# One-core attention and two dense blocks in float32: low words of the float64 weights in PSUM, FF rows in plain order, eight late products on GpSimd, refitted ranks

## The chip, the cores and the metric

The kernel runs on one core of a Trainium2 chip. The metric is the time of one execution on the device in microseconds (us). Three runs of the kernel before were timed, and one more execution was profiled. The engines are named as the profile names them: PE (TensorE), ACT (ScalarE), DVE (VectorE), POOL (GpSimd), SP (SyncE, which here only issues DMAs).

## The reference

```python
# q (1,12288,128), kv (1,384,32,128) float32; alpha (2048), a (4), b (2)
kv_pool = kv.reshape(B, H//4, 4, W//4, 4, C).mean(axis=(2, 4))      # 768 keys
k = v = kv_pool.reshape(B, -1, C) @ w_sr
s = (q @ k.T) / sqrt(C);  a_ = exp(s - max(s));  a_ /= sum(a_) + 1e-9
x = (a_ @ v).reshape(12288, 128)
h = x @ w_in                                                         # 128 -> 2048
x = (max(h, 0) + alpha * min(h, 0)) @ w_out                          # 2048 -> 128
h = x @ w_in2                                                        # 128 -> 2048
P = a[0] + a[1]*h + a[2]*h**2 + a[3]*h**3
Q = 1 + |b[0]|*|h| + |b[1]|*h**2
out = (P / (Q + 1e-6)) @ w_out2                                      # 2048 -> 128
```

The four weight matrices arrive as float64, 512 KB for each slice of 512 of the 2048 FF rows or columns; the rest is float32.

## The kernel before, in words

**Work.** The 12288 query rows are 96 attention tiles of 128. Four tiles make a chunk of 512 rows, which is what both dense blocks work on: 24 chunks, each of 16 steps of 128 FF columns per block. A product that must keep float32 precision is made by `mm3`: both operands are split in a high and a low part in a reduced format, and three matmuls are summed in PSUM.

**First block, a step** (`moe1`): three matmuls into a PSUM bank `h1`, ACT's relu, a split into `rh` and `rl` on ACT and POOL, and matmuls onto `acc1`. The part that is linear in x goes through one 128x128 matrix M, made from the weights once.

**Second block, a pair of steps** (`moe2`, 128x1024 where both steps go together): matmuls into two banks `h2`; `u = |h|` and `p1` on ACT; `t` and `t2` on POOL (Q - 1 by Horner's rule); `ln` and `ex` on ACT give r = 1/Q in the PSUM pair `rp`; on DVE `p2` and `p3` for each step, then `e` = Q r, `gr` = P r (its sign turned) and `g` = (e - 2) gr, a Newton step; PE then adds the two products of `g` to `acc2`. `gr` is written over r in `rp`, which one pair at a time can hold.

**Weights.** `f64_to_f32` takes a float64 slice as pairs of 32-bit words. ACT makes a magnitude of the high words (`mag`) and a float of the low words (`low`, into a buffer `lf`); DVE clamps, shifts, joins the sign (`join`), takes the exponent, scales `lf` with it (`scale`) and adds (`final`). There are 16 slices: four each of w_in and w_out of both blocks. For a w_in slice, ACT and DVE then make the high and the low part (`hi`, `lo`). For the first block PE also transposes the w_in slice and multiplies it with the w_out slice for M; that goes through a PSUM bank `m` with one buffer, which the pooling of kv and the transposes of q use as well. Loads go through a ring `ld` of seven buffers.

**Start.** kv comes in 12 loads of 512 KB. DVE adds pairs of rows, PE pools them by matmuls (L496), and two matmuls (L528) make the keys, of which ACT and DVE write the high and low part (`kTh`, `kTl`, L537). Then the first 12 tiles of attention (`EARLY`) run with wider buffers.

**Order.** All work is first listed as operations with an engine, a cost, a rank and their dependencies. `emit_in_time` then plays a list schedule: on each engine the operation that can start first by the planner's costs is emitted, ties by rank. Buffers are rings whose users are linked in order of rank. What it emits is the fixed order of each engine's queue; on the chip each engine takes its queue in that order and waits by semaphores. The ranks come from tables of numbers (`WR`, `TR`, `RK`, `LH` and others).

Of the kernel before, what the change touches and what calls it, by code (L numbers as in the profile page):

```python
# [196 lines left out]
def kernel(  # L197
# [28 lines left out]
    RT = 11.07  # L226
    RA = 12.85
    RB = 105.28
    SPREAD = 38.43
    WLO = "DVE"  # L230
# [22 lines left out]
    NE = "POOL"  # L253
    NL = "POOL"
    SCL = "DVE"
    FIN = "DVE"
    RK = dict(
        relu=-90.72, G2a=26.46, u=4.12, p1=-20.09, t=-74.51, ln=78.89, ex=26.27, e=150.58, p2=25.63, p3=18.07, gr=-75.87, g=21.27, G2b=19.62, gs=13.78, q=27.79,
# [77 lines left out]
    first = units((("pooled", 2), ("ld", 2), ("bits", 2), ("w", 2), ("wo", 1), ("lf", 1)))  # L336
# [64 lines left out]
    with tc.manual_schedule():  # L401
# [12 lines left out]
        nc.gpsimd.dma_start(out=al.rearrange("p (g k) -> p g k", k=4), in_=moe_alpha.rearrange("(g p k) -> p g k", p=P, k=4))  # L414
# [6 lines left out]
        def queries(c, rank, ring):  # L421
# [38 lines left out]
            ld = add("SP", 1.6 if by_dve else 0.8, rank - 20, load)  # L460
# [128 lines left out]
        def f64_to_f32(src, order, dst, rank, dst_ring=None):  # L589
# [45 lines left out]
            def scale():  # L635
                TT[SCL].tensor_tensor(
# [11 lines left out]
            ld = add("SP", 1.5, rank - 10, load)  # L648
# [3 lines left out]
            lw = add("ACT", act_us(CH, True), rank, low, ld)  # L652
            d_lf = rings["lf"].take(lw)
# [22 lines left out]
        def prep_wo(n, w, g, rank):  # L676
# [4 lines left out]
            def dst():  # L681
# [827 lines left out]
```

## Time and profile before

| | us |
|---|---|
| median of 3 runs | 1550.62 (1547.54 to 1551.07) |
| the profiled execution | 1551.88, of it the span on the core 1549.8 |
| PE busy in the span | 1495.5 (97%) |
| DVE busy | 1448.8 (93%) |
| ACT busy | 1417.3 (91%) |
| POOL busy | 1314.0 (85%) |

Mean granted TensorE clock 0.991. All shares are averages over a start, a long middle and an end, which have different limits. A matmul row overlaps the next, so a mean duration on PE is longer than the distance between starts; on DVE and ACT too a row begins some 0.08 us before the one ahead of it has ended.

### The profile page before, as it was taken

To read this page: it belongs to the slowest core of one execution; us is meant where nothing else is said; L and a number is where in the kernel's file an instruction comes from. 1 tells how busy PE (TensorE), PEld (TensorE's weight loads), DVE (VectorE), ACT (ScalarE), POOL (GpSimd) and SP (SyncE) were. 2 spreads that over 40 slices of the span, in tenths; PEclk is the share of its full clock that TensorE was granted. 3 is DMA by queue.
4 is the path that set the end of the run, shared out by engine and by line. 5 is a ranking of instruction groups with operands and counts; after the bars stand their busy time and mean duration, and the time that the engine had idled before them with its cause. 6 is when DMAs were issued, how large, how long until landed. Compare 5 with 4: busy or idle time off the path is not lost.

```text
span 1549.8 us, 20219 instructions
## 1 busy us (share of the span) xinstructions
PE 1495.5 (97%) x6372; PEld 1074.5 (69%) x6372; DVE 1448.8 (93%) x2171; ACT 1417.3 (91%) x2465; POOL 1314.0 (85%) x1007
## 2 busy tenths in 40 slices
PE   6979999999999999999999999999999999999985
PEld 5866777777777777777777777776777776767642
DVE  6995899999999999999999999999999999999997
ACT  3867999999999999999999999999999999999974
POOL 0456999998999999989999889999899998989763
PEclk9999999999999999999999999999999999999998
DMA  8310000000000000000000000000000000000000
GB/s 274 121 36 1 8 7 8 14 1 15 14 1 15 8 8 8 14 8 15 7 8 15 3 12 8 8 14 7 8 14 7 1 8 7 1 8 7 4 11 7
DMA packets 99211, 28.64 MB, mean 18 GB/s; under 512 B 92929, under 2 KB 95505, under 8 KB 99105
## 3 DMA queue, kind: packets, MB, share of 16 engines
q1 hardware_dynamic: 98976, 27.28, 7.5%
q8 instruction: 50, 0.82, 0.2%
q0 software_dynamic: 128, 0.08, 0.1%
q14 instruction: 57, 0.46, 0.1%
HBM read 21.05 MB, written 6.29 MB: 18 GB/s over the span
## 4 chain that ended last, share of the span: by engine, by line
PE 86%; DVE 7%; ACT 4%; POOL 1%; issue 1%; DMA 1%; SPq 0%; DVEq 0%; ACTq 0%
PE acc L1267 19%; PE h L378 11%; PE h L380 11%; PE h L379 11%; PE acc L1138 6%; PE acc L378 4%; PE acc L380 4%; PE acc L379 4%; PE S L378 4%; PE S L379 4%; PE S L380 4%; PE S L882 3%; PE m L496 1%; DVE work L1234 1%; DVE rp L1228 1%
## 5 line engine op out<-in xcount | busy, mean ns | idle before, releaser
L1191 POOL TENSOR_TENSOR work<-work 128x1024 f32<-128x1024 f32 x192 | 461.2, 2402 | 6.4
L1267 PE MATMUL acc<-work,wo 128*128 128x512 f32 x768 | 393.5, 601 | 18.7 <-DVE work L1234 18.7
L1177 ACT ACTIVATE work<-h,nav 128x512 f32<-128x512 f32 x384 | 316.4, 828 | 19.8 <-PE h L380 17.1
L1122 POOL TENSOR_TENSOR rl<-work,rh 128x512 fp32r<-128x512 f32 x216 | 281.6, 1304 | 39.5 <-ACT rh L1113 36.0
L1184 POOL TENSOR_SCALAR work<-work,bab 128x1024 f32<-128x1024 f32 x192 | 231.3, 1205 | 77.1 <-ACT work L1172 58.5
L1217 DVE TENSOR_TENSOR work<-work,h 128x512 f32<-128x512 f32 x384 | 259.2, 681 | 30.8 <-ACT work L1172 29.1
L1221 DVE SCALAR_TENSOR_TENSOR work<-work,nav,h 128x512 f32<-128x512 f32 x384 | 283.2, 743 | 3.1
L1211 DVE SCALAR_TENSOR_TENSOR work<-work,rp 128x1024 f32<-128x1024 f32 x192 | 233.7, 1217 | 24.8 <-ACT rp L1204 22.0
L1172 ACT ACTIVATE work<-h 128x512 f32<-128x512 f32 x384 | 247.8, 654 | 2.5 <-POOL work L1191 2.0
L1228 DVE SCALAR_TENSOR_TENSOR rp<-work,nav,rp 128x1024 f32<-128x1024 f32 x192 | 246.3, 1283 | 0.0
L1234 DVE SCALAR_TENSOR_TENSOR work<-work,rp 128x1024 f32<-128x1024 f32 x192 | 233.4, 1215 | 2.1
L1101 ACT ACTIVATE work<-h 128x512 f32<-128x512 f32 x336 | 216.3, 644 | 19.7 <-PE h L380 14.2
L1196 ACT ACTIVATE work<-work 128x1024 f32<-128x1024 f32 x192 | 215.2, 1121 | 11.9 <-POOL work L1191 10.0
L1204 ACT ACTIVATE rp<-work 128x1024 f32<-128x1024 f32 x192 | 207.9, 1083 | 9.9 <-DVE work L1234 8.1
L378 PE MATMUL h<-x,w1h 128*128 128x512 f32 x384 | 201.3, 524 | 1.1 <-DVE rl L1105 0.6
L378 PE MATMUL h<-x1h,w2h 128*128 128x512 f32 x384 | 189.8, 494 | 1.1 <-DVE work L1221 1.0
L1267 PEld LDWEIGHTS acc<-work,wo 128*128 128x128 f32 x768 | 139.0, 191 | 66.7 <-DVE work L1234 24.9
L901 POOL TENSOR_TENSOR aTl<-tf,aTh 128x384 fp32r<-128x384 f32 x168 | 170.8, 1021 | 9.2 <-ACT tf L383 9.1
L380 PE MATMUL h<-x1h,w2l 128*128 128x512 f32 x384 | 152.3, 397 | 0.0
L380 PE MATMUL h<-x,w1l 128*128 128x512 f32 x384 | 152.0, 396 | 0.0
L379 PE MATMUL h<-x1l,w2h 128*128 128x512 f32 x384 | 151.9, 396 | 0.0
L379 PE MATMUL h<-x,w1h 128*128 128x512 f32 x384 | 151.5, 395 | 0.0
(133 smaller groups left out, 3220.6 us busy)
## 6 DMA issues: line engine op xcount, KB each, us to landing
work<-in_kv_dram SPq DMA_DIRECT2D x12, 512.0 KB, 7.6
out_dram<-work SPq DMA_DIRECT2D x184, 32.0 KB, 1.6
qraw<-in_q_dram SPq DMA_DIRECT2D x80, 64.0 KB, 2.3
work<-in_moe_w_out_dram SPq DMA_DIRECT2D x8, 512.0 KB, 3.9
work<-in_moe_w_in_dram SPq DMA_DIRECT2D x8, 512.0 KB, 4.4
qraw<-in_q_dram SPq DMA_DIRECT2D x4, 256.0 KB, 3.7
out_dram<-work SPq DMA_DIRECT2D x2, 128.0 KB, 1.8
wsr<-in_w_sr_dram POOLq DMA_DIRECT2D x1, 64.0 KB, 5.5
```

The costliest lines, as they stand in the source:

```text
L378: nc.tensor.matmul(out=ps, lhsT=wh, rhs=xh, start=start, stop=False)
L379: nc.tensor.matmul(out=ps, lhsT=wh, rhs=xl, start=False, stop=False)
L380: nc.tensor.matmul(out=ps, lhsT=wl, rhs=xh, start=False, stop=stop)
L1122: nc.gpsimd.tensor_tensor(out=E["rl", s], in0=E.pop(("r1", s)), in1=E["rh", s], op=ALU.subtract)
L1172: nc.scalar.activation(out=E["u", s][:, k, :], in_=E["h2", s + k], func=AF.Abs)
L1177: nc.scalar.activation(out=E["p1", s][:, k, :], in_=E["h2", s + k], func=AF.Identity, scale=nav[:, 3:4], bias=nav[:, 2:3],)
L1191: nc.gpsimd.tensor_tensor(out=t, in0=t, in1=E.pop(("u", s)), op=ALU.mult)
L1217: nc.vector.tensor_tensor(out=p, in0=p, in1=E["h2", s + k], op=ALU.mult)
L1221: nc.vector.scalar_tensor_tensor(out=p, in0=p, scalar=nav[:, 1:2], in1=E.pop(("h2", s + k)), op0=ALU.add, op1=ALU.mult,)
L1228: nc.vector.scalar_tensor_tensor(out=r, in0=E.pop(("p1", s)), scalar=nav[:, 0:1], in1=r, op0=ALU.add, op1=ALU.mult)
L1234: nc.vector.scalar_tensor_tensor(out=E["g", s], in0=E.pop(("tq", s)), scalar=2.0, in1=E.pop(("r0", s)), op0=ALU.subtract, op1=ALU.mult,)
L1267: nc.tensor.matmul(out=E["acc2", i], lhsT=wo[2][:, KEEP[2].index(j), :], rhs=E["g", s][:, k, :], start=st_, stop=sp,)
```

## The change

It changes five things. The 12 kv loads now stand ahead of all weight loads, by the ranks. The rows of w_out and the columns of w_in keep their plain order: before, column 4n+k of a slice of 512 was put at place 128k+n, so that each partition of w_out was one piece of memory, and the words of w_in were read with a step of eight words; now the step is two words, and w_out comes in four pieces per partition. The low words go to PSUM bank `m`, in place of the SBUF buffer `lf`; for the second block's w_in the sum stays there too, until its low part is made. The early softmax normalization goes from POOL to ACT. Of the last twenty pairs in the second block, the eight that `GEND` marks make `g` by POOL: ACT takes 2 from `e` (L1246), `gr` is written over `p1` in SBUF, and POOL multiplies (L1250). All ranks are new, and some costs of DMA loads in the planner.

```diff
-    WR = (-126.9, 2.81, 54.73, 71.55, 98.56, 110.47, ...)
+    WR = (34.8, 36.79, 93.53, 109.53, 113.01, 193.0, ...)
...
+    GEND = (0, 1, 1, 0, 1, 1, 0, 1, 1, 1, 1, 0, 0, 0, 0, 0, 0, 0, 0, 0)
...
-    NE = "POOL"
+    NE = "ACT"
...
-        nc.gpsimd.dma_start(out=al.rearrange("p (g k) -> p g k", k=4), in_=moe_alpha.rearrange("(g p k) -> p g k", p=P, k=4))
+        nc.gpsimd.dma_start(out=al, in_=moe_alpha.rearrange("(k p) -> p k", p=P))
...
-                nc.sync.dma_start(out=x["raw"], in_=src.bitcast(I32))
-                r2 = x["raw"].rearrange(f"p ({order} w) -> p w k n", w=2, k=4)
-                x["hi"], x["lo"] = r2[:, 1], r2[:, 0].bitcast(U32)
+                nc.sync.dma_start(
+                    out=x["raw"].rearrange("p (k n) -> p k n", k=k), in_=src.bitcast(I32)
+                )
+                r2 = x["raw"].rearrange("p (n w) -> p n w", w=2)
+                x["hi"], x["lo"] = r2[:, :, 1], r2[:, :, 0].bitcast(U32)
...
             def low():
-                x["lf"] = flat("lf")
-                copy(kn(x["lf"]), x["lo"], 2.0 ** -52)
+                x["lf"] = new("aps", "m", [P, CH])
+                copy(x["lf"], x["lo"], 2.0 ** -52)
...
-            d_lf = rings["lf"].take(lw)
+            d_lf = x["d_lf"] = rings["m"].take(lw)
...
+            if t < EARLY and NE == "ACT":
+                copy(A["e", t], A["e", t], A.pop(("r", t)))
+                return
...
         def dve_gr(s):
-            r = E["r0", s]
+            r, p = E.pop(("r0", s)), E.pop(("p1", s))
+            E["gr", s] = p if by_pool(s) else r
             nc.vector.scalar_tensor_tensor(
-                out=r, in0=E.pop(("p1", s)), scalar=nav[:, 0:1], in1=r, op0=ALU.add, op1=ALU.mult
+                out=E["gr", s], in0=p, scalar=nav[:, 0:1], in1=r, op0=ALU.add, op1=ALU.mult
             )
+        def by_pool(s):
+            k = (NS - 2 - s) // 2
+            return k < len(GEND) and GEND[k]
+
+        def act_f(s):
+            t = E["tq", s]
+            nc.scalar.activation(out=t, in_=t, func=AF.Copy, bias=-2.0)
+
+        def pool_g(s):
+            E["g", s] = sb2(s // NB, "g")
+            nc.gpsimd.tensor_tensor(
+                out=E["g", s], in0=E.pop(("tq", s)), in1=E.pop(("gr", s)), op=ALU.mult
+            )
...
+            if by_pool(s):
+                ff = add("ACT", act_us(2 * w, True), stage(s, "f"), lambda: act_f(s), e)
+                gg = add("POOL", pool_us(2 * w), stage(s, "gp"), lambda: pool_g(s), gr, ff)
+                d_p.append(gg)
+                d_r.append(gr)
```

**SP, the start of its queue.** `work<-in_kv_dram` are the kv loads, `work<-in_moe_w_..` the weight slices, `qraw` the queries. Before:

```order
L595 DMA work<-in_moe_w_out_dram 128x1024
L430 DMA qraw<-in_q_dram 128x4x128
L595 DMA work<-in_moe_w_in_dram 128x1024 x2
L480 DMA work<-in_kv_dram 128x1024 x8
L595 DMA work<-in_moe_w_in_dram 128x1024
L480 DMA work<-in_kv_dram 128x1024 x4
```

And with the change:

```order
L429 DMA qraw<-in_q_dram 128x4x128
L479 DMA work<-in_kv_dram 128x1024 x10
L429 DMA qraw<-in_q_dram 128x4x128
L479 DMA work<-in_kv_dram 128x1024 x2
L594 DMA work<-in_moe_w_out_dram 128x4x256
```

Three weight loads that stood ahead of the kv loads, and one between them, now stand behind all twelve.

**DVE, the end of its queue.** This is from the last `p2` on. Before: L1217 is `p2`, L1221 `p3`, L1211 `e`, L1228 `gr`, L1234 `g`.

```order
L1217 TENSOR_TENSOR work<-work,h_14555 128x512
L1211 SCALAR_TENSOR_TENSOR work<-work,rp 128x1024
L1221 SCALAR_TENSOR_TENSOR work<-work,nav,h_14555 128x512
L1228 SCALAR_TENSOR_TENSOR rp<-work,nav,rp 128x1024
L1234 SCALAR_TENSOR_TENSOR work<-work,rp 128x1024
L1211 SCALAR_TENSOR_TENSOR work<-work,rp 128x1024
L1228 SCALAR_TENSOR_TENSOR rp<-work,nav,rp 128x1024
L1234 SCALAR_TENSOR_TENSOR work<-work,rp 128x1024
```

With the change L1223 is `p2`, L1227 `p3`, L1217 `e`, L1235 `gr`, L1256 `g`:

```order
L1223 TENSOR_TENSOR work<-work,h_14570 128x512
L1235 SCALAR_TENSOR_TENSOR work<-work,nav,rp 128x1024
L1227 SCALAR_TENSOR_TENSOR work<-work,nav,h_14570 128x512
L1217 SCALAR_TENSOR_TENSOR work<-work,rp 128x1024
L1235 SCALAR_TENSOR_TENSOR work<-work,nav,rp 128x1024
L1217 SCALAR_TENSOR_TENSOR work<-work,rp 128x1024
L1235 SCALAR_TENSOR_TENSOR rp<-work,nav,rp 128x1024
L1256 SCALAR_TENSOR_TENSOR work<-work,rp 128x1024
```

Of the products in these last rows one is left, and `gr` of the two marked pairs goes to `work` in SBUF.

**POOL, the same end.** With the change L1190 is `t`, L1197 `t2`, L1250 the product; before there is only `t` and `t2` in turn:

```order
L1197 TENSOR_TENSOR work<-work 128x1024
L1250 TENSOR_TENSOR work<-work 128x1024
L1190 TENSOR_SCALAR work<-work,bab 128x1024
L1197 TENSOR_TENSOR work<-work 128x1024
L1190 TENSOR_SCALAR work<-work,bab 128x1024
L1197 TENSOR_TENSOR work<-work 128x1024
L1250 TENSOR_TENSOR work<-work 128x1024 x2
```

The last two marked products stand behind all of POOL's other work; the others stand between `t` and `t2` of later pairs.

## Rows read from the trace of the kernel before

**Rows 1.** Stages: busy us (count) of PE, PEld, DVE, ACT, POOL; clock; DMA share, GB/s

```profile
0.00:14.00 14.00, 1.09 (x4) 0.72 (x4) 6.90 (x16) 6.36 (x7) 3.27 (x10) 1.00 0.81 254
14.00:45.00 31.00, 28.13 (x117) 25.69 (x118) 22.62 (x42) 10.04 (x18) 0.00 (x0) 1.00 0.80 278
45.00:144.00 99.00, 85.56 (x468) 70.26 (x468) 87.72 (x183) 74.28 (x153) 55.07 (x56) 0.97 0.17 46
144.00:1478.00 1334.00, 1333.81 (x5678) 955.81 (x5677) 1270.95 (x1866) 1285.45 (x2233) 1223.49 (x924) 1.00 0.05 9
1478.00:1550.00 72.00, 46.94 (x110) 21.99 (x108) 60.62 (x69) 41.15 (x56) 32.19 (x19) 0.86 0.04 8
```

**Rows 2.** Timeline of PE, 0 to 45 us: start, us, instruction, idle before and releaser

```profile
5.28 1.09 PE L448 MATMUL m<-ident,qraw 128*128 128x128 f32 x4 [5.28 <-DMA qraw<-in_q_dram]
14.11 3.60 PE L496 MATMUL m<-pool_m,work 128*128 128x32 f32 x16 [7.74 <-DVE work L485]
...
30.71 3.62 PE L496 MATMUL m<-pool_m,work 128*128 128x32 f32 x16 [0.56 <-DVE mf L766]
34.70 3.62 PE L496 MATMUL m<-pool_m,work 128*128 128x32 f32 x16 [0.37 <-ACT work L383]
...
42.68 1.65 PE L528 MATMUL S<-work,wsr 128*128 128x384 f32 x2 [0.37 <-ACT work L383]
```

**Rows 3.** Timeline of DVE, around the keys and the second block's first product

```profile
33.24 0.42 DVE L604 TENSOR_SCALAR work<-work 128x512 int32<-128x512 int32 x1
33.58 0.68 DVE L485 TENSOR_TENSOR work<-work 128x512 f32<-128x512 f32 x1
...
44.89 0.56 DVE L537 SCALAR_TENSOR_TENSOR kTl<-S,kTh 128x384 fp32r<-128x384 f32 x1 [0.82 <-ACT kTh L383]
...
143.74 0.69 DVE L1217 TENSOR_TENSOR work<-work,h 128x512 f32<-128x512 f32 x1 [2.42 <-ACT work L1172]
```

**Rows 4.** DVE groups by form, 45 to 144 us, and one line's min/median/max ns

```profile
L636 DVE TENSOR_TENSOR work<-work 128x512 f32<-128x512 f32 x11 | 10.4, 943 | 3.1 <-ACT work L383 2.9
L627 DVE SCALAR_TENSOR_TENSOR work<-work 128x512 int32<-128x512 int32 x10 | 9.2, 930 | 0.0
L643 DVE TENSOR_TENSOR work<-work 128x512 f32<-128x512 f32 x5 | 5.9, 1186 | 0.0
L752 DVE TENSOR_TENSOR work<-m,al x4: 679/686/692, 27.2 to 95.6; 128x512 f32<-128x512 f32 x4
```

**Rows 5.** ACT groups by form, 45 to 144 us, and one line's min/median/max ns

```profile
L383 ACT ACTIVATE work<-work 128x512 f32<-128x512 uint32 x11 | 10.1, 915 | 6.9 <-DVE wo L643 6.9
L857 ACT ACTIVATE e<-e,nm 128x768 f32<-128x768 f32 x4 | 3.7, 929 | 0.4 <-DVE e L850 0.4
L611 ACT ACTIVATE work<-work x16: 656/944/1229, 4.4 to 109.6; 128x512 f32<-128x512 f32 x16
```

**Rows 6.** Timeline around the end: the last chunk's x, the last products

```profile
1480.26 0.69 DVE L1155 TENSOR_TENSOR x1l<-acc,x1h 128x512 fp32r<-128x512 f32 x1
...
1540.74 3.41 PE L1267 MATMUL acc<-work,wo 128*128 128x512 f32 x4 [2.21 <-DVE work L1234]
```

**Rows 7.** Groups from 1480 to 1541 us: busy us, mean ns, idle before

```profile
L1191 POOL TENSOR_TENSOR work<-work 128x1024 f32<-128x1024 f32 x9 | 21.4, 2373 | 0.7
L1234 DVE SCALAR_TENSOR_TENSOR work<-work,rp 128x1024 f32<-128x1024 f32 x10 | 12.1, 1214 | 0.2
L1184 POOL TENSOR_SCALAR work<-work,bab 128x1024 f32<-128x1024 f32 x8 | 9.6, 1195 | 22.6 <-ACT work L1172 22.6
L1196 ACT ACTIVATE work<-work 128x1024 f32<-128x1024 f32 x9 | 9.5, 1059 | 6.6 <-POOL work L1191 6.6
```

**Rows 8.** Waits from 1480 to 1541 us: total, times, longest

```profile
PE acc L1267 <- DVE work L1234: 18.7, 9, 3.7
```

More of the change, by code (lines that the diff above doesn't have):

```diff
@@ L225 @@
     T = 1.0034
[L226 to L230, printed above, removed]
+    RT = 12.15
+    RA = 15.94
+    RB = 117.87
+    SPREAD = 28.11
     WOM = "POOL"
@@ L335 @@
     units = lambda names: [(k, j, n) for k, n in names for j in range(BUFS[k])]
-    first = units((("pooled", 2), ("ld", 2), ("bits", 2), ("w", 2), ("wo", 1), ("lf", 1)))
+    first = units((("pooled", 2), ("ld", 2), ("bits", 2), ("w", 2), ("wo", 1)))
     then = units((("r1", 1), ("y", 1), ("u", 2), ("tq", 2), ("p1", 2), ("r0", 2), ("g", 2)))
@@ L458, in lo @@
                 )
-            ld = add("SP", 1.6 if by_dve else 0.8, rank - 20, load)
+            ld = add("SP", 1.6 if by_dve else 1.0, rank - 20, load)
             d_raw = rings["qraw"].take(ld)
@@ L586, with f64_to_f32 @@
         ]
-        def f64_to_f32(src, order, dst, rank, dst_ring=None):
+        def f64_to_f32(src, k, dst, rank, dst_ring=None):
             x = {}
@@ L635, in scale @@
             def scale():
-                TT[SCL].tensor_tensor(
+                nc.vector.tensor_tensor(
                     out=x["lf"], in0=x["lf"], in1=x["sg"].bitcast(F32), op=ALU.mult
@@ L647, in f64_to_f32 @@
             c1 = 0.335
-            ld = add("SP", 1.5, rank - 10, load)
+            ld = add("SP", 1.8, rank - 10, load)
             d_raw = rings["ld"].take(ld)
@@ L651, in f64_to_f32 @@
             d_bits = rings["bits"].take(a)
-            lw = add("ACT", act_us(CH, True), rank, low, ld)
-            d_lf = rings["lf"].take(lw)
+            lw = add("ACT", act_us(CH), rank, low, ld)
+            d_lf = x["d_lf"] = rings["m"].take(lw)
             c = add("DVE", c1, rank, clamp, a, port=True)
@@ L659, in f64_to_f32 @@
             c = add("DVE", c1, rank, expo, c, port=True)
-            s = add(SCL, tt_us(SCL, CH), rank, scale, c, lw, port=True)
-            f = add(FIN, tt_us(FIN, CH), rank, final, s, port=True)
+            s = add("DVE", dve_us(CH), rank, scale, c, lw)
+            f = add("DVE", dve_us(CH), rank, final, s)
             if dst_ring:
@@ L695, in prep_wo @@
             f, y = f64_to_f32(
-                wo_src(w, g), "k n", dst, rank, "wo" if any(j in SPL[n] for j in js) else None
+                wo_src(w, g), 4, dst, rank, "wo" if any(j in SPL[n] for j in js) else None
             )
@@ L727, in dst @@
             def dst():
+                if n == 2:
+                    return x["lf"]
                 x["ww"] = buf("w", 2)
                 return x["ww"][:, 0, :]
-            f, x = f64_to_f32(wi_src(w, g), "n k", dst, rank, "w")
-            hi = add("ACT", act_us(CH, True), rank, lambda: copy(h[:, sl], x["dst"]), f)
+            f, x = f64_to_f32(wi_src(w, g), 1, dst, rank, "w" if n == 1 else None)
+            hi = add("ACT", act_us(CH, n == 1), rank, lambda: copy(h[:, sl], x["dst"]), f)
             lo = add(
-                WLO, tt_us(WLO, CH), rank,
-                lambda: TT[WLO].tensor_tensor(
+                "DVE", dve_us(CH), rank,
+                lambda: nc.vector.tensor_tensor(
                     out=l[:, sl], in0=x["dst"], in1=h[:, sl], op=ALU.subtract
-                ), hi, port=True,
+                ), hi, port=n == 1,
             )
-            x["d_dst"].append(lo)
+            x["d_dst" if n == 1 else "d_lf"].append(lo)
             w_ready[n][g] = [hi, lo]
@@ L982, in scores @@
             eng = NE if t < EARLY else NL
-            n = add(eng, 0.89 if eng == "POOL" else 0.53, rank, lambda: norm(t), r, port=True)
+            n = add(
+                eng, {"POOL": 0.89, "DVE": 0.53, "ACT": 0.82}[eng], rank, lambda: norm(t), r,
+                port=eng != "ACT",
+            )
             d_r.append(n)
@@ L1416, in moe2 @@
             gr = add("DVE", dve_us(2 * w, 1), stage(s, "gr"), lambda: dve_gr(s), first, p3, ex, e)
-            gg = add("DVE", dve_us(2 * w), stage(s, "g"), lambda: dve_g(s), gr, e)
-            d_p.append(gr)
-            d_r.append(gg)
+            if by_pool(s):
[3 more added lines that the diff above has]
+                d_r.append(gr)
+            else:
+                gg = add("DVE", dve_us(2 * w), stage(s, "g"), lambda: dve_g(s), gr, e)
+                d_p.append(gr)
+                d_r.append(gg)
             d_tq.append(gg)
```

35 lines of the change are left out of this document (16 added, 19 removed).

## The prediction

> **What bounds the kernel now.** I read the stages first, by busy time per engine [rows 1]. From 144 to 1478 us PE is busy 1333.81 of 1334 us at a granted clock of 1.00, so the middle cannot get shorter unless PE gets less work. The change takes no matmul away. What can be won lies in the start, where PE is idle 14.0 - 1.1 = 12.9, 31.0 - 28.1 = 2.9 and 99.0 - 85.6 = 13.4 us, together 29.2, and in the end, where it is idle 72.0 - 46.9 = 25.1 us at a clock of 0.86.
>
> Next, PE's timeline of the start [rows 2]. The first pooling of kv starts at 14.11, after a wait of 7.74 us for DVE's sum, which waits for the load: DMA is moving 254 GB/s and is 0.81 busy [rows 1]. Sixteen pooling matmuls, two kv loads, take 34.70 - 30.71 = 3.99 us; the second half of the keys is multiplied at 42.68. DVE's timeline [rows 3] has the last `kTl` at 44.89 and the first `p2`, with which the steady work begins, at 143.74: 99 us. In these 99 us DVE is busy 87.72, PE 85.56 and ACT 74.28.
>
> Then the end. The last chunk's `x1l` starts at 1480.26, the last product on `acc` at 1540.74 [rows 6], 60.5 us later. DVE is busy 60.62 of the last 72 us [rows 1], nearly all of it in there, while POOL waits 22.6 us for ACT's `u` and ACT 6.6 us for POOL [rows 7]. PE waits 18.7 us for DVE's `g` [rows 8]. So DVE bounds the end.
>
> **Base.** The profiled execution took 1551.88, its span is 1549.8, the difference 2.1 lies outside. The median is 1550.62, 1.26 less. I forecast differences and take them from the median. About 0.3%, 4.65 us, is what a measurement of this kernel can tell from no change.
>
> **The start: kv first.** Before, three weight loads and one of queries, 1.75 MB, are queued ahead of the first kv load. By 5.28 us [rows 2] the first two of these, 0.75 MB, have landed. After, the queries and the first two kv halves are the first 0.75 MB, so the first pooling can start at 5.3 + 0.69 for DVE's sum, about 6.1, 8.0 earlier. Six groups of 3.99 make 23.9 and one product of the keys some 0.8 (half of the 1.65 of [rows 2]): pooling ends near 30.8. All that must arrive, 6.8 MB of kv and queries, needs 24.5 us at the 278 GB/s of [rows 1], near 27 with the slow beginning, so PE and not the DMA sets this. Before, products for M stood among the pooling; they move behind it. The last `kTl` then comes at about 34 instead of 45.4 (its end), 11.5 earlier. The vector `al` is now read with a stride of one float, a slower DMA on POOL's queue; nothing before shows such a load. It is needed only after the keys; if it took bandwidth from kv it could delay by up to some 2 us, and I take 0.
>
> **The work behind it.** What is no longer done before the keys must be done between keys and first `p2`. By the order of DVE's queue there are there 10 more TENSOR_SCALARs at a distance of 0.34 [rows 3], 3.4 us, and 11 more full-width rows (4 joins, 3 scales, a final, a product with `al`, a `lo`, an `rl`) at 0.69 - 0.08 = 0.6, 6.6 us; the short rest comes to -0.3. Together +9.7. Against that, plain order and the PSUM operand save. `scale` costs 943 and `final` 1186 ns on the mean, while L752, with the same size and an operand in PSUM, costs 686 with hardly any spread [rows 4]. I take that: 11 x 0.257 = 2.8 and 5 x 0.5 = 2.5. `join` costs 930 at a step of eight words; I take 686 here too, 10 x 0.244 = 2.4. DVE: 87.7 + 9.7 - 7.7 = 89.7. If none of these savings came it would be 97.4; nothing in the rows lets them be larger.
>
> The Trainium skill, "SBUF — State Buffer", section "Who interferes with whom", says that a VectorE instruction with two SBUF inputs contends with a GpSimd one that reads SBUF, and one with a single SBUF input doesn't. By that rule `scale` and `final` do lose their surplus, but `join`, which keeps both inputs in SBUF, may keep all of its own: the 2.4 would be gone, and DVE would be at 92.1, the sum below 2.4 higher.
>
> ACT gets 5 more `mag` at about 0.7 (3.5), 3 more `low` (2.1), and the 12 normalizations at some 0.85 (the nearest is L857, 929 ns for the same 768 elements [rows 5], less the overlap), 10.2, and loses some 3 of other rows that now stand elsewhere: +12.8. `low` falls from 915 toward the 656 that an ACT row of this size takes at best, 11 x 0.26 = 2.8, `mag` likewise by 2.3. ACT: 74.3 + 12.8 - 5.1 = 82.0. PE gets one product for M more, 1.7: 87.3. POOL loses the normalizations, and was at 55.07 of 99.
>
> The busiest engine grows from 87.7 to 89.7, 2%. If the stage keeps its ratio of 99 to 87.7, it grows by 2.3, to 101.3. The first `p2` comes 11.5 - 2.3 = 9.2 earlier: **-9**. Bounds: 0, if the stage takes all 11.5 back (from 99 to 110.5, which its engines' sums allow for); about -18, if the reshuffled order brought the stage down to what its busiest engine needs, near 90.
>
> **The middle.** PE's work is the same, so 0, as long as it never starves. The cover is thin: ACT is busy 1285 and DVE 1271 of 1334 [rows 1]. Lengthening by 1% would be 13 us.
>
> **The end: products to POOL.** Behind the last `x1l` ten `g` are left on DVE before [rows 7]. After, seven of these are POOL's. DVE loses 7 x (1.214 - 0.08) = 7.9: 60.6 - 7.9 = 52.7. POOL gets eight products at 2.37 (its `t2` has the same form [rows 7]), 19: 32.2 + 19 = 51.2. ACT gets seven `f` at 1.06 [rows 7]: 41.2 + 7.4 = 48.6. `e` and `gr` stay on DVE. For a pooled pair POOL works 1.20 + 2.37 + 2.37 = 5.9 us, as long as the 6.0 us in which a pair passes now (60.5 / 10). Three engines nearly level, each waiting for the others twice in a pair, don't run gapless; I take a little over half of DVE's gain, **-4.5**. Bounds: -7.9, and +8, if a pooled pair passes at POOL's 5.9 plus a wait of about 1.2 for `f`, seven times over.
>
> **Sum.** -9.2 - 4.5 = -13.7, and 1550.6 - 13.7 = **1537**.
>
> **Rivals.**
> 1. *POOL becomes the bound of the end*, chance 0.14. For it: the product takes 2373 ns there against 1214 on DVE, and the 5.9 us per pooled pair above. Against it: POOL idles 22.6 us there, and only part of the pairs are marked. The end gains nothing: 1550.6 - 9.2 = 1541.4. The Trainium skill, "GPSIMD Engine Reference", section "4.1 Engine selection", gives elementwise work to VectorE because GPSIMD is about twice as slow with two inputs; the trace's two durations agree (1.95). By that rule the products should have stayed.
> 2. *The start gives back what it wins*, chance 0.13: from the keys on the work is set by queues, with DVE, ACT and PE all at 82 to 90 us. The stage grows by 11.5, and -4.5 is left: 1546.
> 3. *Slower: bank `m`*, chance 0.11. It has one buffer, and now holds low words from `low` to `final` (for w_in of the second block to `lo`) while products for M, transposes and queries need it too. Sixteen conversions each hold it. The chain runs from the keys at 34 to about the first `p2` of before, 143.7 [rows 3]; other users of the bank take an estimated 25 us of that (for each of four slices the transposes, the product with `al` and the matmuls for M, and the queries' transposes, at 0.7 to 1.7 us each). So it decides from an average hold of (143.7 - 34 - 25) / 16 = 5.3 us. If holds average 1 us above that, conversions end 16 us later, and with them the first steps: about 1566. Against it: in DVE's order `scale` and `final` stand at most three rows apart. Starvation of PE in the middle, 1%, would give about the same time, and I count it here.
>
> **Chances.** The forecast 0.62, the rivals as above. Faster by over 0.3% is below 1546: the forecast's 0.62, all but a little of rival 1 (0.13) and little of rival 2, about 0.76. Same, 1546 to 1555: most of rival 2, 0.13. Slower: 0.11. The range goes from 1527, where the start yields 15 and the end all of 7.9, to 1551, behind rival 2.
>
> **What would show it.** In the changed kernel's profile: first pooling near 6 us, the last `kTl` near 33, the first `p2` near 134.5; `scale` at 0.69 with no spread; `join` tells row and rule apart (0.69 or above 0.9). PE is again fully busy in the middle at clock 1.00. From the last `x1l` to the last product about 56 us, with DVE's busy time near 53 and POOL's near 51. I would be wrong if `low` on ACT waits for bank `m` for tens of us, if PE shows waits over 10 us between 144 and 1478, or if PE in the end waits for POOL's product as long as it does for `g` now.

## The result, and the profile after

| | before | changed |
|---|---|---|
| median, us | 1550.39 (4 runs) | 1531.32 (1530.59 to 1532.16, 4 runs) |
| ratio | | 0.9881, 95% interval 0.9863 to 0.9898 |
| span of the profiled execution, us | 1549.8 | 1529.3 |

The kernel became 19.1 us faster; 13.6 were forecast, and the range held the time. By the profiles the span fell by 20.5. I divide it at three rows: DVE's last `kTl`, the first `p2`, the last `x1l`. The windows of the changed kernel between them, with the columns of [rows 1] (the last three are clock, DMA share, GB/s):

```profile
6.80:36.00 29.20, 25.27 (x104) 23.04 (x105) 10.30 (x17) 3.66 (x10) 0.00 (x0) 1.00 0.76 251
36.10:128.30 92.20, 84.58 (x474) 71.49 (x473) 86.87 (x202) 79.83 (x167) 41.05 (x43) 0.98 0.30 83
128.30:1463.90 1335.60, 1335.56 (x5687) 958.67 (x5686) 1283.02 (x1883) 1290.19 (x2246) 1227.65 (x926) 1.00 0.05 9
1463.90:1529.30 65.40, 44.94 (x108) 20.59 (x106) 51.14 (x59) 47.74 (x62) 49.34 (x25) 0.88 0.04 9
```

| | before | changed | difference | forecast |
|---|---|---|---|---|
| last `kTl` starts | 44.9 | 36.1 | -8.8 | -11.5 |
| from there to the first `p2` ("the stage") | 98.8 | 92.2 | -6.6 | +2.3 |
| first `p2` to last `x1l` | 1336.6 | 1335.6 | -1.0 | 0 |
| last `x1l` to the end of the span | 69.5 | 65.4 | -4.1 | -4.5 |

So the end and the middle went as forecast, the keys came later than forecast, and the stage behind them, which was to grow, shrank. In the stage DVE was busy 87.6 of 98.8 us before, idle 11.2; now it is busy 86.9 and idle 5.3, though it does twenty rows more (202 against 182).

PE's timeline of the start (answering to [rows 2]) shows why the keys are late. The first pooling starts at 6.89, where the prediction had 6.1. The third load (eight matmuls) is pooled at 10.84, but the fourth only at 14.40: PE waits 1.64 us for DVE's sum, that is for the load, where the prediction had twelve loads pooled without a gap.

```profile
6.89 3.59 PE L495 MATMUL m<-pool_m,work 128*128 128x32 f32 x16 [2.06 <-DVE work L484]
10.84 1.91 PE L495 MATMUL m<-pool_m,work 128*128 128x32 f32 x8 [0.37 <-ACT work L382]
14.40 1.92 PE L495 MATMUL m<-pool_m,work 128*128 128x32 f32 x8 [1.64 <-DVE work L484]
...
33.91 1.65 PE L527 MATMUL S<-work,wsr 128*128 128x384 f32 x2 [0.37 <-ACT work L382]
```

DVE's and ACT's groups in the stage, 36.1 to 128.3 us (answering to [rows 4, 5]): `scale` (L634) is at 693 ns where it was 943, as forecast with hardly any spread, `final` (L641) at 679 to 695 in its full-width rows, `join` (L625) at a mean of 833 but a median of 684, `low` (uint32) at 650 and `mag` (L609) at 682; the normalization takes ACT 955 ns.

```profile
L602 DVE TENSOR_SCALAR work<-work 128x512 int32<-128x512 int32 x27 | 12.1, 462 | 0.0
L625 DVE SCALAR_TENSOR_TENSOR work<-work 128x512 int32<-128x512 int32 x14 | 11.7, 833 | 0.0
L634 DVE TENSOR_TENSOR m<-m,work 128x512 f32<-128x512 f32 x14 | 9.7, 693 | 1.3 <-ACT m L382 1.3
L602 DVE TENSOR_SCALAR work<-work 128x512 f32<-128x512 f32 x14 | 6.1, 443 | 0.0
L641 DVE TENSOR_TENSOR work<-work,m 128x512 f32<-128x512 f32 x4 | 2.7, 679 | 0.0
L382 ACT ACTIVATE e<-e,r 128x768 f32<-128x768 f32 x12 | 11.3, 955 | 0.2 <-DVE r L869 0.2
L609 ACT ACTIVATE work<-work 128x512 f32<-128x512 f32 x14 | 9.4, 682 | 0.0
L382 ACT ACTIVATE m<-work 128x512 f32<-128x512 uint32 x14 | 9.1, 650 | 2.7 <-DVE wo L641 1.9 <-DVE work L641 0.5
```

`scale` and `join` again, with the shortest, median and longest row in ns, up to 140 us:

```profile
L634 DVE TENSOR_TENSOR m<-m,work x16: 681/692/700, 39.4 to 136.7; 128x512 f32<-128x512 f32 x16
L625 DVE SCALAR_TENSOR_TENSOR work<-work x16: 673/684/1760, 31.4 to 133.6; 128x512 int32<-128x512 int32 x16
```

The end's groups (1463 to 1526 us, answering to [rows 7, 8]) have eight products on POOL and three on DVE. PE now waits 7.0 us for POOL's product and hardly for DVE's.

```profile
L1289 PE MATMUL acc<-work,wo 128*128 128x512 f32 x58 | 31.4, 676 | 7.3 <-POOL work L1250 7.0 <-DVE work L1256 0.3
L1197 POOL TENSOR_TENSOR work<-work 128x1024 f32<-128x1024 f32 x9 | 21.3, 2367 | 0.4
L1250 POOL TENSOR_TENSOR work<-work 128x1024 f32<-128x1024 f32 x8 | 19.0, 2374 | 0.6 <-DVE work L1235 0.4 <-issue 0.2
L1190 POOL TENSOR_SCALAR work<-work,bab 128x1024 f32<-128x1024 f32 x9 | 10.8, 1195 | 4.7 <-ACT work L1178 4.4
L1256 DVE SCALAR_TENSOR_TENSOR work<-work,rp 128x1024 f32<-128x1024 f32 x3 | 3.7, 1217 | 0.1
```

### The profile page after: what moved, and what is told of

It is laid out like the page before. It is cut to its first block, busy times and chain, and to the rows that moved or that the text cites. A ratio compares the mean times of both kernels' runs of the same rounds, so it can differ in the third digit from the quotient of the medians.

```text
span 1529.3 us, 20231 instructions
## 1 busy us (share of the span) xinstructions
PE 1491.5 (98%) x6372; PEld 1074.6 (70%) x6372; DVE 1433.2 (94%) x2163; ACT 1423.4 (93%) x2485; POOL 1321.7 (86%) x1003
## 4 chain that ended last, share of the span: by engine, by line
PE 91%; DVE 4%; ACT 2%; POOL 2%; issue 1%; DMA 1%; SPq 0%; POOLq 0%; ACTq 0%; DVEq 0%
PE acc L1289 21%; PE h L377 12%; PE h L379 11%; PE h L378 11%; PE acc L1144 6%; PE acc L377 4%; PE acc L379 4%; PE acc L378 4%; PE S L377 4%; PE S L378 4%; PE S L379 4%; PE S L885 4%; PE m L495 1%; POOL work L1250 1%; DMA work<-in_kv_dram 1%
## 5 line engine op out<-in xcount | busy, mean ns | idle before, releaser
L1197 POOL TENSOR_TENSOR work<-work 128x1024 f32<-128x1024 f32 x192 | 460.6, 2399 | 8.3
L1227 DVE SCALAR_TENSOR_TENSOR work<-work,nav,h 128x512 f32<-128x512 f32 x384 | 283.8, 743 | 4.6
L1223 DVE TENSOR_TENSOR work<-work,h 128x512 f32<-128x512 f32 x384 | 259.9, 681 | 24.6 <-ACT work L1183 23.6
L1190 POOL TENSOR_SCALAR work<-work,bab 128x1024 f32<-128x1024 f32 x192 | 231.2, 1204 | 44.6 <-ACT work L1178 32.7
L1217 DVE SCALAR_TENSOR_TENSOR work<-work,rp 128x1024 f32<-128x1024 f32 x192 | 233.5, 1216 | 17.0 <-ACT rp L1210 13.4
L1178 ACT ACTIVATE work<-h 128x512 f32<-128x512 f32 x384 | 239.8, 631 | 10.1 <-PE h L379 8.0
L1235 DVE SCALAR_TENSOR_TENSOR rp<-work,nav,rp 128x1024 f32<-128x1024 f32 x184 | 235.8, 1281 | 0.0
L1256 DVE SCALAR_TENSOR_TENSOR work<-work,rp 128x1024 f32<-128x1024 f32 x184 | 223.4, 1214 | 1.7
L1107 ACT ACTIVATE work<-h 128x512 f32<-128x512 f32 x336 | 211.4, 630 | 11.9 <-PE h L379 9.2
L1202 ACT ACTIVATE work<-work 128x1024 f32<-128x1024 f32 x192 | 211.2, 1100 | 8.8 <-POOL work L1197 6.6
L377 PE MATMUL h<-x1h,w2h 128*128 128x512 f32 x384 | 193.1, 503 | 8.2 <-DVE work L1227 8.1
## 6 DMA issues: line engine op xcount, KB each, us to landing
out_dram<-work SPq DMA_DIRECT2D x2, 128.0 KB, 1.8
```

The costliest lines, as they stand in the source:

```text
L377: nc.tensor.matmul(out=ps, lhsT=wh, rhs=xh, start=start, stop=False)
L1178: nc.scalar.activation(out=E["u", s][:, k, :], in_=E["h2", s + k], func=AF.Abs)
L1197: nc.gpsimd.tensor_tensor(out=t, in0=t, in1=E.pop(("u", s)), op=ALU.mult)
L1217: nc.vector.scalar_tensor_tensor(out=t, in0=t, scalar=QEPS, in1=E["r0", s], op0=ALU.add, op1=ALU.mult)
L1223: nc.vector.tensor_tensor(out=p, in0=p, in1=E["h2", s + k], op=ALU.mult)
L1227: nc.vector.scalar_tensor_tensor(out=p, in0=p, scalar=nav[:, 1:2], in1=E.pop(("h2", s + k)), op0=ALU.add, op1=ALU.mult,)
```

## The experiments

Two theories stood against each other for the 6 us by which the stage shrank where it was to grow. **A**: the new order of the conversions spreads them better. **B**: the three mechanical parts (low words in PSUM, normalizations on ACT, plain row order) make DVE's rows shorter than I had worked out. To keep order out of it, six kernels leave every queue's order as in the changed kernel and only swap an engine, a buffer, a layout or a load at the place where an instruction is issued.

Five profiles share the changed kernel's start (the changed kernel itself, e1, e5, e11 and e12): their first `p2` is at 128.3, 130.8, 128.0, 130.6 and 130.3, mean 129.6; their stages are 92.2, 93.5, 91.1, 93.7 and 93.6, mean 92.8, with DVE busy 87.5 on the mean. Stage differences below are against these means and carry about 1 us of scatter.

| run | ratio to before (95%) | last `kTl` | first `p2` | stage | DVE busy in it |
|---|---|---|---|---|---|
| changed | 0.9881 (0.9863 to 0.9898) | 36.1 | 128.3 | 92.2 | 86.9 |
| e2 normalizations on POOL | 0.9921 (0.9909 to 0.9933) | 36.8 | 135.1 | 98.3 | 92.8 |
| e3 low words in SBUF | 1.0065 (1.0053 to 1.0077) | 36.7 | 138.6 | 101.9 | 96.3 |
| e5 control of e3 | 0.9979 (0.9969 to 0.9988) | 36.9 | 128.0 | 91.1 | 86.9 |
| e4 old row order | 0.9941 (0.9928 to 0.9954) | 35.1 | 136.3 | 101.2 | 93.8 |
| e9 all three undone | 1.0121 (1.0106 to 1.0136) | 37.3 | 147.2 | 109.9 | 102.0 |
| e10 kv behind other loads | 0.9922 (0.9910 to 0.9935) | 42.7 | 134.9 | 92.2 | 87.7 |
| e6 new ranks alone | 1.0181 (1.0157 to 1.0206) | 35.6 | 170.2 | 134.6 | 106.2 |
| e7 old start ranks | 1.0111 (1.0097 to 1.0124) | 51.4 | 138.3 | 86.9 | 75.2 |
| e8 kv loads first, alone | 1.0228 (1.0214 to 1.0242) | 64.7 | 174.7 | 110.0 | 91.1 |

**e1, the end without POOL's products.**

```diff
-    GEND = (0, 1, 1, 0, 1, 1, 0, 1, 1, 1, 1, 0, 0, 0, 0, 0, 0, 0, 0, 0)
+    GEND = (0, 0, 0, 0, 0, 0, 0, 0, 0, 0, 0, 0, 0, 0, 0, 0, 0, 0, 0, 0)
```

> The changed kernel with all of GEND at zero, so that every product g stays on DVE. If the end's 4.1 us (63.9 before, 59.8 after, from the last x1l to the end of the last product) come from DVE's unloading, the stretch goes back to about 64 and the time rises by 4, to 1535.5; everything ahead of the last x1l stays as it is. If the end was shorter for another reason (the refitted ranks of the second block), the time stays within 1 us of 1531.3. If pooled products hold the end up, it falls.

Measured: 1538.32, ratio 0.9931 (0.9918 to 0.9944). From the last `x1l` the end takes 69.2 us, 3.8 more than with the products, and DVE is busy 58.8 of them again:

```profile
1467.30:1536.50 69.20, 44.80 (x108) 21.41 (x106) 58.76 (x68) 40.42 (x54) 30.59 (x17) 0.88 0.04 8
```

So the products on POOL are worth the end's gain. The rest of this run's distance lies in work that the edit doesn't touch (first `p2` 2.5 us later, middle 0.8 longer); the five profiles of that start differ by up to 2.8 us at the first `p2`.

**e2, the normalizations back on POOL, same order.**

```diff
-            if t < EARLY and NE == "ACT":
-                copy(A["e", t], A["e", t], A.pop(("r", t)))
-                return
-            TT[NE if t < EARLY else NL].tensor_scalar(
+            TT[NL].tensor_scalar(
```

> The changed kernel with every queue in the same order, but the 12 early normalizations emitted on POOL instead of ACT at the same places. Theory A (the stage between keys and first p2 lost its waits by the order of the conversions and the full-rate DVE rows): ACT gets 11 us of room that it does not need, POOL has room too; the first p2 moves by under 1.5 us, time 1531 to 1533. Theory B (the softmax chain through POOL was what made the stage wait): the first p2 comes 4 to 6 us later, time about 1536.

Measured: 1536.49; stage +5.5, the size that the expectation gives for theory B, but not by the softmax chain that it names. PE waits only 0.2 us for POOL's normalization. DVE pays instead: its own rows got longer in the same window (36.8 to 135.1 us), the TENSOR_SCALARs (clamp, shift and exponent) from 462 and 443 to 562 and 568 ns, `join` from 833 to 896, `w1l` from 730 to 886. That is 27 x 0.100 + 14 x 0.125 + 14 x 0.063 + 4 x 0.156 = 6.0 us, about all of the stage's growth.

```profile
L602 DVE TENSOR_SCALAR work<-work 128x512 int32<-128x512 int32 x27 | 14.8, 562 | 0.0
L625 DVE SCALAR_TENSOR_TENSOR work<-work 128x512 int32<-128x512 int32 x14 | 12.5, 896 | 0.0
L602 DVE TENSOR_SCALAR work<-work 128x512 f32<-128x512 f32 x14 | 7.9, 568 | 0.0
L735 DVE TENSOR_TENSOR w1l<-work,w1h 128x512 fp32r<-128x512 f32 x4 | 3.5, 886 | 0.0
```

A normalization on POOL was thus paid for on DVE, in longer rows that no view lists as a wait. The timelines of POOL and DVE, put together, show it row by row: a TENSOR_SCALAR takes 0.41 us while POOL idles, and 1.05 or 0.88 beside a normalization (L872).

```profile
59.12 1.33 POOL L872 TENSOR_SCALAR e<-e,r 128x768 f32<-128x768 f32 x1
59.67 1.05 DVE L602 TENSOR_SCALAR work<-work 128x512 f32<-128x512 f32 x1
62.77 0.41 DVE L602 TENSOR_SCALAR work<-work 128x512 int32<-128x512 int32 x1
67.36 0.91 POOL L872 TENSOR_SCALAR e<-e,r 128x768 f32<-128x768 f32 x1 [6.92 <-DVE r L869]
67.67 0.88 DVE L602 TENSOR_SCALAR work<-work 128x512 int32<-128x512 int32 x1
```

The Trainium skill, "SBUF — State Buffer", section "Who interferes with whom", says that VectorE's TENSOR_SCALAR in its two-port modes contends with GpSimd for a shared port pair, and an instruction with two SBUF inputs with a GpSimd one that reads SBUF. The trace agrees: these are the rows that grew, and `scale` with its PSUM operand stayed at 689. In which mode the TENSOR_SCALARs ran, no run shows.

**e3 and e5, the low words in SBUF, and the control for the room.** The `tf` ring of attention gives up its third buffer for the `lf` buffer; e5 has only this.

```diff
-                x["lf"] = new("aps", "m", [P, CH])
+                x["lf"] = at.tile([P, CH], F32, tag="lf", name="lf", bufs=1)
...
+        if tag == "tf":
+            k %= 2
```

> The changed kernel with every queue in the same order, but the low words in an SBUF buffer instead of a PSUM bank, with the same holds (and the tf ring of attention at two buffers instead of three, for the room). Theory A1 (DVE's scale and final ran long because both inputs lay in SBUF): scale and final go from 0.69 to a mean of 0.85 to 1.2, DVE gets 5 to 8 us more in the stage, first p2 4 to 7 us later, time 1535 to 1538. Theory A2 (order alone did it): scale may get longer, but the first p2 moves by under 1.5 us and the time stays at 1531 to 1533.

> The control of the run with low words in SBUF: the changed kernel, same order, only the tf ring of attention at two buffers instead of three. If that ring caused the 18 us by which the middle grew there (1361 us from first to last x1l against 1343), this kernel has the 18 us too and takes about 1549, with its first p2 within 2 us of 130; then the low words in SBUF are worth what is left, 8 us at the first p2. If the SBUF buffer itself slowed the middle, this one takes 1531 to 1533.

Measured: e3 1558.22, e5 1547.00. e5 has the changed kernel's start, and a middle that is 16.4 us longer (1352.0; PE waits 8.3 us in it for `tf`). So that part of e3 belongs to `tf`. The low words in SBUF cost the stage 9.1, and DVE 8.8: `scale` has a mean of 856, `final` into `wo` one of 1181, and the TENSOR_SCALARs go to 555 and 491. A2 falls. A1 holds for 5.5 of DVE's us, the rows of `scale` and `final`; another 3.2 are TENSOR_SCALARs, which the edit doesn't touch, and which have longer rows here only beside POOL (table behind e9).

```profile
L604 DVE TENSOR_SCALAR work<-work 128x512 int32<-128x512 int32 x27 | 14.7, 555 | 0.0
L636 DVE TENSOR_TENSOR lf<-lf,work 128x512 f32<-128x512 f32 x14 | 12.0, 856 | 1.4 <-ACT lf L384 1.4
L643 DVE TENSOR_TENSOR wo<-work,lf 128x512 f32<-128x512 f32 x4 | 4.7, 1181 | 0.1
```

**e4, the old row order, same queues.** Put back are the load in one piece, `kn` for the outputs of `mag`, `low` and `join`, and alpha in fours.

```diff
-                nc.sync.dma_start(
-                    out=x["raw"].rearrange("p (k n) -> p k n", k=k), in_=src.bitcast(I32)
-                )
-                r2 = x["raw"].rearrange("p (n w) -> p n w", w=2)
-                x["hi"], x["lo"] = r2[:, :, 1], r2[:, :, 0].bitcast(U32)
+                nc.sync.dma_start(out=x["raw"], in_=src.bitcast(I32))
+                r2 = x["raw"].rearrange(f"p ({k} w) -> p w k n", w=2, k=4)
+                x["hi"], x["lo"] = r2[:, 1], r2[:, 0].bitcast(U32)
...
-                copy(x["lf"], x["lo"], 2.0 ** -52)
+                copy(kn(x["lf"]), x["lo"], 2.0 ** -52)
```

> The changed kernel with every queue in the same order, but rows and columns of the weights permuted as before (one piece of memory per partition of w_out, words of w_in read at a step of eight words, alpha in pieces of four). If the step of eight words was a price on ACT and DVE, mag and low go from 0.67 to about 0.9 and join from 0.83 to 0.95, some 8 us of ACT and 2 of DVE, first p2 1 to 4 us later, time 1532 to 1535. If it was not, all three keep their length and the time stays at 1531.

Measured: 1538.84; stage +8.4, twice the expectation's upper end. ACT's `mag` is at 959 and `low` at 910, `join` at 1035, so reading words at a step of eight and writing them in four strips had its price on ACT, 14 x (0.277 + 0.260) = 7.5 us, and on `join`, 2.8. Which of the two steps costs what, no run separates. DVE's other 3.5 us are mostly TENSOR_SCALARs, 3.2 more than in the changed kernel, again beside POOL.

```profile
L626 DVE SCALAR_TENSOR_TENSOR work<-work 128x512 int32<-128x512 int32 x14 | 14.5, 1035 | 0.0
L382 ACT ACTIVATE m<-work 128x512 f32<-128x512 uint32 x15 | 13.7, 910 | 2.1 <-DVE wo L642 1.3 <-DVE work L642 0.6
L610 ACT ACTIVATE work<-work 128x512 f32<-128x512 f32 x14 | 13.3, 959 | 0.0
```

**e9, all three undone at once, same order** (the edits of e2, e3 and e4 together).

> The changed kernel with every queue in the same order, but all three mechanical parts undone together: low words in SBUF (tf at two buffers for the room, which alone adds 16 us to the middle), normalizations on POOL, the old row order. One by one they cost 10.8, 6.0 and 8.9 us in the stage between the keys and the first p2. If DVE's busy time rules, the costs add: stage 92.3 + 25.7 = 118, first p2 at 154, later than the 143.7 of before, time 1570 to 1576. If they overlap (each ran into the same waits), the stage is 102 to 110 and the time 1555 to 1563.

Measured: 1568.7, between the two cases; stage 109.9, at the upper end of the second, +17.1, DVE +14.5. So the three overlap: alone they cost 5.5 + 9.1 + 8.4 = 23.0. (The 10.8 that the expectation has for the low words is too high: e3's stage is 9.7 above the changed kernel's.) The first `p2` is at 147.2, 3.5 us later than in the kernel before, although the keys come 7.6 us earlier.

```profile
37.30:147.20 109.90, 91.86 (x478) 75.45 (x477) 102.00 (x202) 80.04 (x157) 58.24 (x56) 0.94 0.24 70
```

The TENSOR_SCALARs tell what the runs have in common. There are 41 of them in each of these stages. Sorted by whether a POOL instruction runs during any of their time, they have these lengths in ns:

| run | POOL busy in the stage, us | with POOL: count, mean, longest | without: count, mean, longest |
|---|---|---|---|
| changed | 41.0 | 19, 500, 1147 | 22, 418, 423 |
| e2 | 52.6 | 25, 660, 1522 | 16, 413, 421 |
| e3 | 43.9 | 15, 740, 1510 | 26, 414, 422 |
| e4 | 40.3 | 13, 786, 1503 | 28, 417, 451 |
| e9 | 58.2 | 21, 776, 1509 | 20, 418, 434 |

Without POOL the length hardly varies; all of the growth is beside POOL. How much POOL has to do is only a part of it: in e3 and e4 POOL has about as much as in the changed kernel, and fewer rows meet it, but these are longer. Why these meetings cost more is not settled.

**e10, what kv first is worth by itself.** Three loads of 512 KB that nothing reads go ahead of kv, into room that is free then.

```diff
+            if (b, h) == (0, 0):
+                for z in range(3):
+                    t = (wo[2][:, 0:8], wo[2][:, 8:16], work[:, 31:33])[z].rearrange("p a b -> p (a b)")
+                    nc.sync.dma_start(out=t, in_=kvv[z])
```

> The changed kernel with every queue in the same order, but three more loads of 512 KB (copies of kv that nothing reads) ahead of the kv loads in SP's queue, as many as the weight loads that stood there before. It measures kv first by itself. By the step on record the keys come 1.5 MB / 278 GB/s = 5.7 us later and everything behind them too: first p2 at 134, time 1536 to 1538. If the stage behind the keys could make up for late keys (it is bounded by conversions whose loads come after), the first p2 moves by under 2 us and the time stays at 1531 to 1533.

Measured: 1538.7; the keys at 42.7, 5.9 later than the mean of the five, the first `p2` 5.3 later, the stage unchanged at 92.2. In this order nearly all of a delay of the keys passes on to the first `p2`, as the prediction has it; the time is a little above the 1536 to 1538 expected. The estimate of 5.7 from 278 GB/s comes out, though not by its path: the first pooling starts 8.5 us later than in the changed kernel (15.35 against 6.89), and then the pooling runs without waiting for a load and makes up for some of it.

**e6, e7, e8, parts of the tables with another order.** These let the planner set a new order.

```diff
e6 (before):  all ranks of the changed kernel (WR, TR, LH, LM, LT, RT, RA, RB, SPREAD, RK)
e7 (changed): WR, TR, LH, LM, LT of before
e8 (before):
-                l = add("SP", 1.35, b + 0.5 * h, lambda b=b, h=h: load_kv(b, h))
+                l = add("SP", 1.35, -300 + b + 0.5 * h, lambda b=b, h=h: load_kv(b, h))
```

> The kernel before with all ranks of the changed one (kv first with them), but its own row order, low words in SBUF, normalizations on POOL and no products on POOL. Theory B (the stage behind the keys is as long as DVE's busy time plus 5 us, and DVE's rows are long wherever POOL works beside them): kv first brings the keys to 36, DVE has 97 us or more to do behind them, first p2 at 138 to 142, time 1543 to 1549. Theory A (the order of the conversions is what pays): first p2 near 132, time 1537 to 1540.

> The changed kernel with the start's ranks of before (WR, TR, LH, LM, LT), so that the weight loads stand ahead of kv again; row order, PSUM low words, ACT's normalizations and POOL's products stay. Theory B: the keys come at 45 again, but DVE's work behind them falls from 87 to 75 or 77, so the first p2 comes at 130 to 134 and the time is 1533 to 1538: the mechanical parts keep most of the gain without kv first. Theory A: the first p2 stays at 140 to 144 and only the end's 4 us are left, 1545 to 1548.

> The kernel before with one edit: the kv loads stand ahead of all other loads in SP's queue. On record the keys were to come 11.5 us earlier and 2.3 of that were to be given back, -9 alone. Theory B: without the relief DVE has 9.7 us more to do behind the keys, so nearly all is given back: first p2 at 140 to 144, time 1546 to 1550. If the step on record holds by itself, first p2 at 135, time 1541.

Measured: 1576.53, 1567.51 and 1585.48, all slower than before and outside every expectation. In e6 the keys come at 35.6 as wanted, but the stage is 134.6 with DVE busy 106.2 and idle 28.4. e9 has nearly the same mechanical parts and start in another order: 109.9, idle 7.9. So order alone is worth some 20 us of DVE's idle time, and the new ranks paid here only together with the parts that they came with. In e7 theory B's number for DVE comes out (75.2 busy in the stage, 75 to 77 expected), in part by luck: about 3.7 of the 12.4 us by which it fell from the kernel before are rows, of softmax mostly, that lie outside the stage there (168 rows in it against 182). The keys come at 51.4, and the middle is 22 us longer, spread over its length; why, I have not settled. e8 shows a mechanism: the loads came first, but not the bank. `m` has one buffer whose users are linked by rank, and there the product M of the first weight slice still stands between the two halves of kv's pooling:

```profile
30.06 1.65 PE L528 MATMUL S<-work,wsr 128*128 128x384 f32 x2 [0.37 <-ACT work L383]
46.20 1.09 PE L748 MATMUL m<-ident,work 128*128 128x128 f32 x4 [14.50 <-DVE work L643]
...
50.56 3.62 PE L496 MATMUL m<-pool_m,work 128*128 128x32 f32 x16 [0.38 <-DVE mf L766]
```

PE waits 14.50 us for a weight whose load now comes after kv. So e8 is no test of kv first; e10 is.

**e11 and e12, two tries at a shorter end.**

```diff
e11:
-    GEND = (0, 1, 1, 0, 1, 1, 0, 1, 1, 1, 1, 0, 0, 0, 0, 0, 0, 0, 0, 0)
+    GEND = (0, 1, 1, 1, 1, 1, 0, 1, 1, 1, 1, 0, 0, 0, 0, 0, 0, 0, 0, 0)
e12:
-            E["gr", s] = p if by_pool(s) else r
+            E["gr", s] = p if (NS - 2 - s) // 2 < len(GEND) else r
...
+                end = (NS - 2 - s) // 2 < len(GEND)
+                d_p.append(gg if end else gr)
+                d_r.append(gr if end else gg)
```

> The changed kernel with a ninth product on POOL: the fourth pair from the end, at a place where POOL was idle for 1.9 us while ACT waited 1.7 us for DVE's product. If the chain ex, e, gr, g over the one rp buffer is what passes there, the end gets 0.5 to 1.5 us shorter (time 1530 to 1531); if POOL bounds the end, it gets 1 to 3 us longer.

> The changed kernel with gr written over p1 in SBUF for all of the last twenty pairs, also for those whose product stays on DVE, so that rp comes free at gr and not at g. If the rp chain limits the end, it gets 1 to 3 us shorter (time 1528 to 1530); if DVE's own work limits it, nothing changes or the products, now with two SBUF inputs beside a busy POOL, get longer (1531 to 1534).

Measured: e11 1534.97, ratio 0.9901 (0.9887 to 0.9914), the end 67.4, 2.0 longer (the seven profiles with the changed kernel's end, itself, e2 to e5, e9 and e10, have 64.9 to 65.8). POOL's timeline shows that the last `t2` (L1197) now stands behind two products more and ends at 1520.80, 53.7 us after the last `x1l` at 1467.1 (before the edit 1513.86, 50.0 us after 1463.9); then DVE waits 3.40 us for its last r.

```profile
1516.13 2.36 POOL L1250 TENSOR_TENSOR work<-work 128x1024 f32<-128x1024 f32 x1
1518.43 2.37 POOL L1197 TENSOR_TENSOR work<-work 128x1024 f32<-128x1024 f32 x1
1520.76 2.35 POOL L1250 TENSOR_TENSOR work<-work 128x1024 f32<-128x1024 f32 x1
```

e12: 1545.93, ratio 0.9970 (0.9958 to 0.9982); the end is 66.9, and the stretch ahead of it some 10 us longer, in which DVE's products of the last pairs lie. With two SBUF inputs they have a median of 1826 ns and reach 2907; with `gr` in PSUM they stay within 1181 and 1226:

```profile
L1256 DVE SCALAR_TENSOR_TENSOR work<-work,rp x172: 1181/1217/1226, 147.2 to 1404.8; 128x1024 f32<-128x1024 f32 x172
L1256 DVE SCALAR_TENSOR_TENSOR work<-work x12: 1185/1826/2907, 1411.1 to 1534.5; 128x1024 f32<-128x1024 f32 x12
```

Neither beats the changed kernel, and no other run does.

## Why the prediction was right, and where it was off

The sign, the range and the places held. That the sum came as near as it did is in part luck: against the forecast the keys came 2.7 us too late, and the stage behind them 8.9 us too short. By steps:

- **The middle, 0.** Right: -1.0, PE idle 0.0 of 1335.6.
- **The end, -4.5.** Right: -4.1 in the profile, 3.8 when taken back (e1). DVE came to 51.1 (52.7 forecast), POOL to 49.3 (51.2), ACT to 47.7 (48.6), over a window that begins 2.3 us later than the prediction's. A little over half of DVE's gain was the right share. Rival 1, POOL as the bound, begins at the ninth product (e11). The Trainium skill, "GPSIMD Engine Reference", section "4.1 Engine selection", has the durations right (2374 against 1217), but its choice of engine would here have cost 3.8 us: what counts is which engine the others wait for.
- **The start, kv first.** The last `kTl` came 8.8 us earlier instead of 11.5: "PE and not the DMA sets this" was wrong for the first loads. The first pooling came 0.8 later than forecast, the wait for a load inside the pooling cost 1.9, and the keys' first product 1.3 instead of 0.8. That the keys' time passes through was right (e10). The vector `al` was put at 0: it takes 8.2 us from issue to landing instead of 6.6, and with its old layout the keys come at 35.1 (e4) and 37.3 (e9) against the mean of 36.8, so no cost stands out of the scatter.
- **The work behind the keys, +2.3.** This step failed: it was -6.0 by the five profiles. Its sum for DVE, 89.7, is near the 87.5 measured, but by two errors that cancel. The added rows were priced at undisturbed lengths (0.34 and 0.60 us), while such rows run longer in that stage: at the new order without the mechanical parts the TENSOR_SCALARs have means of 606 and 593 ns, `join` 1060, and DVE is busy 102.0 (e9), not 97.4. In the kernel before, such rows already had a mean of 565 in that stage (45 to 144 us):

```profile
L604 DVE TENSOR_SCALAR work<-work 128x512 int32<-128x512 int32 x21 | 11.5, 565 | 0.0
```

And the saving was not 7.7 but 14.5 (e9). For the rows that the prediction looked at, its prices were near: `scale` and `final` 5.5 (e3) where 5.3 were booked, `join` 2.8 (e4) where it was 2.4. What it put at nothing is what the parts do to DVE's other rows. Undoing a part makes the TENSOR_SCALARs alone longer by 4.4 (e2), 3.2 (e3) and 3.2 us (e4), by 6.0 together. So the normalizations, booked as a price on ACT alone, freed DVE of 5.2 (e2), the low words of 8.8 (e3) and the row order of 6.3 (e4), each undone alone. The rule that the prediction quotes has no contention for a VectorE instruction with one SBUF input; the TENSOR_SCALARs have one, and e2 has them up by 100 and 125 ns. On ACT the row order gave 7.5 instead of 5.1.

- **"If the stage keeps its ratio of 99 to 87.7."** It didn't. DVE's idle time fell from 11.2 to 5.3. Before, DVE was idle 8.9 of the last 26.7 us ahead of the first `p2`, after it had been busy 23.5 of the 24 from 93 to 117; the changed order has no such heap (idle 2.6 of the last 26.3). In all runs with the changed start's order the idle time lies between 4.2 (e5) and 7.9 (e9), while DVE's work varies by 15 us; in e6, another order with nearly e9's parts, it is 28.4. That the idle time goes mainly with the order is therefore shown; which of the ranks does it is not.
- **`join`, row or rule.** I took 686; the rule quoted there would have left it at 930. The mean, 833, lies between, and both are right in part: the 8 rows of the stage with no POOL instruction beside them have a mean of 681, the 6 others 1036, up to 1760.

Of the rivals, the second (the start gives back what it wins) is what the new order does without the mechanical parts: e9's first `p2` is 3.5 us later than before, with the keys 7.6 earlier. Theory B explains the stage, by DVE's lengths and not by the softmax chain, and theory A's order is its condition: with the parts the same order brings 147.2 down to 129.6. Rival 3 had no weight here (ACT waited 2.7 us for bank `m` in the stage), but e8 shows its mechanism at 14.5 us.

## What to carry to other kernels

When a stage is bound by VectorE, count what GpSimd does beside it: an operation taken off GpSimd, or an operand moved to PSUM, can shorten VectorE's rows without any wait that a profile shows; look for the spread between a row's shortest and mean length, and for what GpSimd runs beside the long rows. Price work that is moved into such a stage at the lengths that rows have there, not at their shortest. And test a part of a change that a scheduler rearranges with the order held fixed: e6, e7 and e8 measured their new orders more than the part they were meant for.

## What the runs showed of the hardware

VectorE's TENSOR_SCALAR of 128x512, with one tensor input, goes from a mean of 462 to 562 ns when GpSimd gets 11.6 us more to do in a stage of 92 to 98 us (e2). With no GpSimd instruction beside it such a row took at most 451 ns in five profiles, beside one up to 1522. A 128x1024 product on VectorE has a median of 1217 ns with an operand in PSUM, and 1826, at most 2907, with both in SBUF (e12); with the operand in PSUM none of 172 takes over 1226, though a GpSimd instruction runs beside 170 of them. ACT's conversion of 512 words takes 650 ns reading at a step of two words and 910 reading at a step of eight and writing in four strips (e4).
